# A fused attention and two-layer-block kernel: the second unit of w_out and the first block's y change places at the start of the third stage

## The chip, the cores and the metric

The kernel runs on one core of a Trainium2 chip. The metric is the device time in microseconds of one execution. A core has a matrix engine (TensorE, PE in the profile, with its weight loads as PEld), a vector engine (VectorE, DVE), a scalar engine (ScalarE, ACT), GpSimd (POOL) and a sync engine (SyncE, SP) that issues nearly all of this kernel's transfers.

## The reference

All inputs are float32, random. Attention is followed by two feed-forward blocks over 2304 tokens:

```python
scores = q @ k.T / 8                # 4 batches, 8 heads, 576 positions, 64 wide
scores = where(mask, scores, -1e9)  # heads 0-3: the last 32 positions; 4-7: every 32nd
x = softmax(scores) @ v             # reordered to (2304, 512)
h = ((x @ w1) * (x @ w2)) @ w3      # 512 -> 1024 -> 1024
y = h @ w_out                       # 1024 -> 512
h = y @ moe2_w_in                   # 512 -> 2048
g = h * sigmoid(1.702 * h)
out = g @ moe2_w_out                # 2048 -> 512
```

## The kernel before

**Numbers.** Every float32 operand is split into a high and a low part of type fp32r (`split_hi` on ScalarE, line 246; `split_lo` on VectorE, line 252), and a product is three matmuls (`ORDER`). Weights arrive as 64-bit words, which are turned into float32 by two ScalarE operations (a scaled copy of each half) and three VectorE operations.

**Stages.** The first two stages do attention, fold `w3` with the first `w_out`, and compute the first block for batches 0 to 2. The result y goes to DRAM (`ydram`). The third stage (`steps3`) does the first block for batch 3: for each half `hb` of its tokens eight passes `m`. A pass is two groups of twelve matmuls (`first`, line 716; places `at` and `at + 1`), a copy of the first group's sum (`copy`, `abf`, ScalarE, at + 0.99), a multiply (`mult`, VectorE, at + 1.99) and the split of the product into `ab` (at + 2.4, at + 2.75). Their PSUM tiles come from a pool of four (`mm`), so a group can start when the group four before it was copied or multiplied. Passes stand at 24 hb + 2 m; at 24 hb + 16 the product with the folded weight follows (`fourth`, line 1352). Places -8 to 0 hold the last such product of batch 2 (line 1173).

Beside these matmuls the third stage prepares the fourth: (a) the first block of y (768 tokens) in two halves `kk`: `y_load` fetches a half, and the nine steps of `y_steps` form sums and split them into `yq`; (b) the second `w_out` in eight units: `wo_load(u)` fetches 1 MB, and the fourteen steps of `wo_steps` convert it (two ScalarE, three VectorE operations), form sums and differences of its quarters, split them and store both parts in `tdram`. Unit 0 is done in the second stage, units 1 to 6 in the third, and unit 7 in the fourth. A unit's high parts are written over its raw tile, the low parts over the half of `sums` that holds the sums; so a raw tile is free when its store has ended. Raw tiles are lent by three rooms: `cv_a`'s `raw` and `x`, and `cv_b`'s `raw`. The second step of `y_steps` needs `x` too.

The fourth stage multiplies y with `w_in` units (`W[n]`, fetched from `widram`, split by ScalarE and VectorE) and the result, after the gelu, with the units in `tdram`, in three blocks of eight quads (`Quad`) and a sweep. A quad is 7 products (line 1496) and 2 pieces (line 1507). The `tdram` units come through a ring of eight tiles (`t_more` issues the next k loads). In a quad ScalarE copies partial sums out of PSUM (`keep`: s1, u1, z1; line 1559), and the next product into the same PSUM tile waits for that copy.

**Order.** Each stage is a list of (place, function). `written` sorts the list by place and emits the functions in that order; each engine then runs its own instructions strictly in that order, and SP its transfers. The places don't delay anything: an engine goes on as soon as its next instruction's inputs, and its output's room, are free. The third stage's places are groups of twelve matmuls; the fourth's are about a microsecond (a quad is 9.49).

At the end of the second stage `early_y` (line 1282) opens the pool `cv_a` and starts both loads of y: half 0 into `cv_a`'s raw tile, half 1 into one half of `sums`. `yq` is in a pool opened after the pools of the second stage (`cv`, `xbs`) were closed.

Of the kernel before, what the change touches and what calls it, by code (L numbers as in the profile page):

```python
# [16 lines left out]
I64 = mybir.dt.int64  # L17
# [4 lines left out]
P = 128  # L22
# [22 lines left out]
CW2 = 1024  # L45
# [4 lines left out]
NU = 8  # L50
# [162 lines left out]
def body(ctx: ExitStack, tc, qk, vv, mask, ql, vl, qs, vs, qmask, w1, w2, w3t, wo, win, wout, out):  # L213
    nc = tc.nc

    def pool(name, bufs=1, stack=ctx, **kw):
        return stack.enter_context(tc.tile_pool(name=name, bufs=bufs, reuse_waits="tile", **kw))
# [100 lines left out]
    def room(what, n, w, tag, bufs):  # L318
        if what + str(n) in lent:
            return lent[what + str(n)]  # L320
        return aq.tile([P, w], F32, tag=tag, name=tag, bufs=bufs)
# [186 lines left out]
    at = aps = None  # L508
# [760 lines left out]
    cv_a = None  # L1269
    early = {}  # L1270
    ys = {}

    def y_load(b, kk, room=None):
        t = room() if room else cv_a.tile([P, CW2], I64, tag="raw", name="raw")
        t = t.bitcast(F32)[:, :2 * BT]
        nc.sync.dma_start(
            t.rearrange("p (h n) -> p h n", h=2),
            ydram[kk::2, :, b * BT:(b + 1) * BT].rearrange("h p n -> p h n"),
        )
        return t  # L1280

    def early_y():
        nonlocal cv_a
        right0.close()
        cv_a = pool("cva", stack=right1, side="right")
        early["sums"] = cv_a.tile([P, 2, 7 * 256], F32, tag="hl", name="sums")
        ys[0] = y_load(0, 0)
        ys[1] = y_load(0, 1, lambda: early["sums"][:, 0])

    def early_load():  # L1290
# [3 lines left out]
    def early_room():  # L1294
        if 1 not in early:
            early[1] = cv[0].tile([P, 2 * CW2], F32, tag="x", name="x", bufs=2)
        return early[1]

    steps2 += [(27.0, early_load), (38.6, early_y)]
    steps2 += [(EARLY_AT + g, f) for g, f in wo_steps(0, lambda: early[0], early_room, None, 1.6)]  # L1300
    written(steps2)
# [8 lines left out]
    def y_steps(kk, ts):  # L1310

        q = {}

        def begin():
            q.update({n: ts[kk][:, n * HT:(n + 1) * HT] for n in range(4)})

        def first_two():
            begin()
            x = q["x"] = cv_a.tile([P, 2 * CW2], F32, tag="x", name="x")[:, :4 * HT]
            q.update({4 + n: x[:, n * HT:(n + 1) * HT] for n in range(4)})  # L1320
            t = ts[kk].rearrange("p (n t) -> p n t", t=HT)
            nc.vector.tensor_tensor(
                x.rearrange("p (m n t) -> p n m t", n=2, t=HT)[:, 0], t.rearrange("p (n m) t -> p m n t", m=2)[:, 1], t[:, :2], op=ALU.subtract,
            )

        def sum_(o, l, r, op):
            nc.vector.tensor_tensor(q[o], q[l], q[r], op=op)

        out = [first_two, lambda: sum_(5, 4, 3, ALU.subtract), lambda: sum_(7, 2, 5, ALU.add)]
        for lo, hi, src in ((0, 1, lambda: q[0]), (1, 3, lambda: ts[kk][:, 2 * HT:]), (3, 7, lambda: q["x"])):  # L1330
            view = lambda src=src: src().rearrange("p (n t) -> p n t", t=HT)
            out.append(lambda lo=lo, hi=hi, view=view: split_hi(yq[:, lo:hi, kk, 0], view()))
            out.append(lambda lo=lo, hi=hi, view=view: split_lo(yq[:, lo:hi, kk, 1], view(), yq[:, lo:hi, kk, 0]))
        return out
# [32 lines left out]
    steps3 = [(at - 48, f) for at, f in over]  # L1367
    for hb in range(2):
# [5 lines left out]
    rooms = (  # L1374
        lambda: cv_a.tile([P, CW2], I64, tag="raw", name="raw"),
        lambda: cv_b.tile([P, CW2], I64, tag="raw", name="raw"),
        lambda: cv_a.tile([P, CW2], I64, tag="x", name="x"),
    )
    sums = early["sums"]
    for kk, at in ((0, -4.6), (1, -1.6)):  # L1380
        gaps = (0.05, 1.0, 1.4, 0.1, 0.75, 0.8, 1.85, 2.0, 2.85)
        steps3 += [(at + g, f) for g, f in zip(gaps, y_steps(kk, ys))]

    todo3 = {}

    def wo_load(u):
        todo3[u] = rooms[(1, 0, 2)[(u - 1) % 3] if u < NU - 1 else 0]()
        nc.sync.dma_start(todo3[u], wout[u])

    UNIT = 7.2  # L1390
    for u in range(1, NU):
        at = 0.6 + UNIT * (u - 1)
        if u < NU - 1:
            steps3.append(((-7, -1.5, 1.4)[u - 1] if u < 4 else at - 2 * UNIT + 0.2, lambda u=u: wo_load(u)))
        if u < NU - 1:
            steps3 += [(at + g, f) for g, f in wo_steps(u, lambda u=u: todo3[u], lambda u=u: sums[:, u % 2])]
    for n, (lo, hi, a, b, c) in enumerate(((4, 6, 32.1, 40.2, 41.6), (5, 7, 40.05, 46.9, 47.7))):
# [47 lines left out]
    def do(at, f, *args, **kw):  # L1445
        steps4.append((at, lambda: f(*args, **kw)))
# [88 lines left out]
    QUAD = 7 * MM + 2 * PC  # L1535
# [144 lines left out]
    late = [f for _, f in wo_steps(NU - 1, lambda: todo3[NU - 1], todo3_lo, todo3_hi)]  # L1680
    at_late = (1.65, 2 + 1.65 / QUAD)
    for f, (i, t) in zip(late, (
        (1, 1.7), (2, 1.7), (2, 3.5), (2, 3.6), (3, 3.5), (3, 3.6), (4, 3.5), (4, 3.55),
        (4, 9.2), (5, 1.7), (5, 3.5), (5, 3.55), (5, 3.6), (5, 5.9),
    )):
        do(i * QUAD + t, f)
# [2 lines left out]

    do(-0.9, t_more, 2)  # L1690
    do(-0.8, W[2].fetch_in_place)
    do(-0.7, t_more, 2)
    do(-0.6, W[3].fetch_in_place)
    do(-0.55, wo_load, NU - 1)
    do(-0.5, t_more, 4)
    for b in range(NB):
        X, Y = [None] * 2, [None] * 2

# [6 lines left out]
        for i in range(NU):  # L1705
            q = Quad(b, i, X, Y, q)
            n = b * NU + i
            at = b * BLOCK + i * QUAD
# [46 lines left out]
```

## Time and profile before

| what | us |
|---|---|
| median of 3 runs | 808.64 (806.70 to 808.92) |
| the profiled execution | 806.77 |
| its span | 805.0 |
| TensorE busy in it | 774.4 |
| VectorE busy | 580.6 |
| ScalarE busy | 480.5 |

The mean granted TensorE clock is 0.992 of full speed. The profile gives the busy time of each engine, the chain of work that ended last, and for idle time of an engine what ended it. "L716" is line 716 of the kernel; `ps<-xal,w` is an instruction that writes `ps` and reads `xal` and `w`. SPq is SP's transfer queue; a transfer's row there is the time of its issue, not of its landing.

### The profile page before, as it was taken

How to read it: one execution, taken by the hardware profiler on the slowest of the kernel's cores; microseconds unless marked ns; L12 is line 12 of the kernel's file. 1: busy time of each engine (PE TensorE's matmuls, PEld its weight loads, DVE VectorE, ACT ScalarE, POOL GpSimd, SP SyncE). 2: the span in 40 equal slices, each digit the busy share in tenths (PEclk: the TensorE clock that was granted, in tenths of full speed). 3: DMA queues.
4: the chain of work that ended last, by engine and by line, in shares of the span. 5: the costliest groups of instructions: out<-in, count | busy, mean ns of one | idle time of the engine just before them, and what ended most of it. 6: DMA issues, size and time to landing. Idle time of an engine off the chain costs nothing.

```text
span 805.0 us, 16757 instructions
## 1 busy us (share of the span) xinstructions
PE 774.4 (96%) x6545; PEld 750.4 (93%) x6545; DVE 580.6 (72%) x1248; ACT 480.5 (60%) x1041; POOL 5.8 (1%) x14
## 2 busy tenths in 40 slices
PE   5899999999999999979999699999999999999997
PEld 4899999978999999879999699999999999999997
DVE  4999678788787787948785487796566795567743
ACT  5878565576665465444565467774566673666552
POOL 2000000000000000000000000000000000000000
PEclk9999999999999999999999899999999999999999
DMA  8976555541877463477999626789444489343382
GB/s 274 322 283 223 199 156 184 177 156 58 278 260 268 160 218 135 152 197 204 237 292 254 267 89 204 305 291 348 159 171 161 147 286 370 128 151 118 116 271 85
DMA packets 72062, 168.14 MB, mean 209 GB/s; under 512 B 6320, under 2 KB 45232, under 8 KB 69424
## 3 DMA queue, kind: packets, MB, share of 16 engines
q1 hardware_dynamic: 71840, 167.04, 62.4%
q8 instruction: 51, 0.84, 0.4%
q14 instruction: 27, 0.22, 0.1%
q10 hardware_dynamic: 144, 0.04, 0.0%
HBM read 130.88 MB, written 36.18 MB: 208 GB/s over the span
## 4 chain that ended last, share of the span: by engine, by line
PE 77%; DMA 8%; DVE 8%; ACT 4%; issue 2%; SPq 1%; ACTq 0%; DVEq 0%
PE acc L1507 22%; PE ps L1496 21%; PE ps L716 16%; PE ps L1173 8%; PE acc L1352 3%; PE acc L1019 3%; DMA raw<-in_w 2%; DMA w<-tdram 1%; DMA tdram<-x 1%; PE sc L533 1%; DVE w L252 1%; DVE xw L809 1%; PE pv L602 1%; DMA abdram<-abf 1%; ACT w L246 1%
## 5 line engine op out<-in xcount | busy, mean ns | idle before, releaser
L1507 PE MATMUL acc<-w,sp 128*128 128x256 f32 x1512 | 188.8, 283 | 0.0
L1507 PEld LDWEIGHTS acc<-w,sp 128*128 128x128 f32 x1512 | 186.7, 191 | 0.4 <-DVE sp L252 0.4
L1496 PE MATMUL ps<-yq,hl 128*128 128x384 f32 x924 | 167.9, 335 | 0.0
L1496 PEld LDWEIGHTS ps<-yq,hl 128*128 128x128 f32 x924 | 158.7, 188 | 0.6 <-DVE part L1452 0.6
L252 DVE TENSOR_TENSOR sp<-part,sp 128x384 fp32r<-128x384 f32 x144 | 75.5, 554 | 69.3 <-ACT sp L246 69.3
L716 PE MATMUL ps<-xah,w 128*128 128x288 f32 x512 | 103.2, 297 | 0.0
L716 PE MATMUL ps<-xbh,w 128*128 128x288 f32 x512 | 102.5, 295 | 0.3 <-DVE w L252 0.2
L716 PEld LDWEIGHTS ps<-xah,w 128*128 128x128 f32 x512 | 82.9, 190 | 0.0
L716 PE MATMUL ps<-xal,w 128*128 128x288 f32 x256 | 77.3, 302 | 5.8 <-ACT abf L1234 3.4
L1173 PE MATMUL ps<-ab,w 128*128 128x288 f32 x576 | 81.0, 300 | 1.8 <-DVE ab L252 1.8
L716 PEld LDWEIGHTS ps<-xbh,w 128*128 128x128 f32 x512 | 81.9, 188 | 0.8 <-DVE w L252 0.7
L1173 PEld LDWEIGHTS ps<-ab,w 128*128 128x128 f32 x576 | 78.3, 192 | 3.2 <-DVE ab L252 2.3
L246 ACT ACTIVATE sp<-part 128x384 fp32r<-128x384 f32 x144 | 68.3, 518 | 16.4 <-PE acc L1507 15.7
L716 PE MATMUL ps<-xbl,w 128*128 128x288 f32 x256 | 77.0, 301 | 0.0
L1449 ACT ACTIVATE part<-part 128x384 f32<-128x384 f32 x72 | 37.8, 526 | 60.5 <-DVE part L1452 60.5
L716 PEld LDWEIGHTS ps<-xal,w 128*128 128x128 f32 x256 | 48.5, 190 | 7.4 <-ACT abf L1234 3.7
L246 ACT ACTIVATE ab<-abf 128x288 fp32r<-128x288 f32 x64 | 27.3, 439 | 42.4 <-DVE abf L1237 40.0
L716 PEld LDWEIGHTS ps<-xbl,w 128*128 128x128 f32 x256 | 48.1, 188 | 0.9
L1019 PE MATMUL acc<-w,w 128*128 128x512 f32 x192 | 45.5, 396 | 0.2
L1019 PEld LDWEIGHTS acc<-w,w 128*128 128x128 f32 x192 | 35.9, 189 | 9.1 <-ACT raw L1025 1.0
L252 DVE TENSOR_TENSOR hl<-fetched,hl 128x1024 fp32r<-128x1024 f32 (+1 forms) x40 | 43.3, 1083 | 0.0
L246 ACT ACTIVATE w<-xw 128x512 fp32r<-128x512 f32 (+1 forms) x30 | 23.2, 774 | 29.6 <-DVE xw L809 28.8
(189 smaller groups left out, 1095.6 us busy)
## 6 DMA issues: line engine op xcount, KB each, us to landing
w<-tdram SPq DMA_DIRECT2D x84, 512.0 KB, 4.2
fetched<-widram SPq DMA_DIRECT2D x20, 896.0 KB, 7.7
raw<-in_win SPq DMA_DIRECT2D x8, 1024.0 KB, 5.5
widram<-x SPq DMA_DIRECT2D x8, 896.0 KB, 5.5
raw<-in_wout SPq DMA_DIRECT2D x6, 1024.0 KB, 6.3
tdram<-sums SPq DMA_DIRECT2D x6, 896.0 KB
raw<-in_w3t SPq DMA_DIRECT2D x10, 512.0 KB, 4.8
abf<-abdram SPq DMA_DIRECT2D x32, 144.0 KB, 4.2
```

The source lines that it names most:

```text
L246: nc.scalar.activation(hi, src, AF.Copy)
L252: e.tensor_tensor(lo, src, r(hi), op=ALU.subtract)
L533: nc.tensor.matmul(sc[:nq, g, i * P:i * P + nk], qs[rows, i], ks[rows, i], start=True, stop=True,)
L602: nc.tensor.matmul(pv[rows, h // 2, :nq], L["v"][:nk, h * D:(h + 1) * D], ps[:nk, h * nq:(h + 1) * nq], start=True, stop=True,)
L716: nc.tensor.matmul(ps, ws[a][m // 2][:, at:at + P], xh[c][:, k, cols], start=(k == 0 and (a, c) == ORDER[0]), stop=(k == KC - 1 and (a, c) ...
L809: "e": lambda xf, rf, ri, ru, x, hi, lo: nc.vector.tensor_tensor(x, x, ri[:, :, 0], op=ALU.add),
L1019: nc.tensor.matmul(acc[f], hl[:, a, f * P:(f + 1) * P], wor[c][g], start=(g == 0 and (a, c) == ORDER[0]), stop=(g == MC - 1 and (a, c) == ...
L1173: nc.tensor.matmul(yacc[n], wfs[a][k][:, n * P:(n + 1) * P], hold[s % 2, k][:, c], start=(k == 0 and (a, c) == ORDER[0]), stop=(k == MC - ...
L1352: nc.tensor.matmul(st[0], wfs[a][k][:, n * P:(n + 1) * P], hold[hb, k][:, c], start=(k == 0 and (a, c) == ORDER[0]), stop=(k == MC - 1 and ...
L1449: nc.scalar.activation(out(), src(), func)
L1496: nc.tensor.matmul(ps, w[a][:, f * 256 + kk * P:f * 256 + (kk + 1) * P], yq[:, b, kk, c], start=(first and kk == 0 and (a, c) == ORDER[0]) ...
L1507: nc.tensor.matmul(to, g.t[:, a, t * P:(t + 1) * P], t3[:, i % 2, c], start=(opens and i == 0 and n == 0 and t % 2 == 0), stop=(i == NU - ...
```

## The change

The load of unit 1 takes the place, in `early_y`, that the load of y's half 0 had, and the tile. Y's half 0 is loaded at place -6.9 of the third stage into `cv_b`'s raw tile, where unit 1's load had been at -7. Unit 1's steps move from 0.6 to -5.8. Y's half 1 is worked first, from -0.9 (it was the second, from -1.6), and half 0 from 2.2 (it was the first, from -4.6). Units 2 to 6 stand at 6 + 7.2 (u - 2), that is 1.8 places earlier, and their loads have new places and rooms.

At the start of the fourth stage the load of unit 7 stands before that of `W[3]`, and the third to sixth ring loads stand behind both. Unit 7's first conversion goes from place 1.7 to 9.2 of quad 1.

```diff
--- before.py
+++ after.py
@@ -1269,6 +1269,7 @@
     cv_a = None
     early = {}
     ys = {}
+    todo3 = {}
 
     def y_load(b, kk, room=None):
         t = room() if room else cv_a.tile([P, CW2], I64, tag="raw", name="raw")
@@ -1284,7 +1285,8 @@
         right0.close()
         cv_a = pool("cva", stack=right1, side="right")
         early["sums"] = cv_a.tile([P, 2, 7 * 256], F32, tag="hl", name="sums")
-        ys[0] = y_load(0, 0)
+        todo3[1] = cv_a.tile([P, CW2], I64, tag="raw", name="raw")
+        nc.sync.dma_start(todo3[1], wout[1])
         ys[1] = y_load(0, 1, lambda: early["sums"][:, 0])
 
     def early_load():
@@ -1377,21 +1379,20 @@
         lambda: cv_a.tile([P, CW2], I64, tag="x", name="x"),
     )
     sums = early["sums"]
-    for kk, at in ((0, -4.6), (1, -1.6)):
+    steps3.append((-6.9, lambda: ys.update({0: y_load(0, 0, rooms[1])})))
+    for kk, at in ((1, -0.9), (0, 2.2)):
         gaps = (0.05, 1.0, 1.4, 0.1, 0.75, 0.8, 1.85, 2.0, 2.85)
         steps3 += [(at + g, f) for g, f in zip(gaps, y_steps(kk, ys))]
 
-    todo3 = {}
-
     def wo_load(u):
-        todo3[u] = rooms[(1, 0, 2)[(u - 1) % 3] if u < NU - 1 else 0]()
+        todo3[u] = rooms[(0, 1, 2, 0, 1, 0)[u - 2]]()
         nc.sync.dma_start(todo3[u], wout[u])
 
     UNIT = 7.2
     for u in range(1, NU):
-        at = 0.6 + UNIT * (u - 1)
-        if u < NU - 1:
-            steps3.append(((-7, -1.5, 1.4)[u - 1] if u < 4 else at - 2 * UNIT + 0.2, lambda u=u: wo_load(u)))
+        at = -5.8 if u == 1 else 6 + UNIT * (u - 2)
+        if 1 < u < NU - 1:
+            steps3.append((((2.6, 5.5, 5.7)[u - 2] if u < 5 else at - 10), lambda u=u: wo_load(u)))
         if u < NU - 1:
             steps3 += [(at + g, f) for g, f in wo_steps(u, lambda u=u: todo3[u], lambda u=u: sums[:, u % 2])]
     for n, (lo, hi, a, b, c) in enumerate(((4, 6, 32.1, 40.2, 41.6), (5, 7, 40.05, 46.9, 47.7))):
@@ -1680,7 +1681,7 @@
     late = [f for _, f in wo_steps(NU - 1, lambda: todo3[NU - 1], todo3_lo, todo3_hi)]
     at_late = (1.65, 2 + 1.65 / QUAD)
     for f, (i, t) in zip(late, (
-        (1, 1.7), (2, 1.7), (2, 3.5), (2, 3.6), (3, 3.5), (3, 3.6), (4, 3.5), (4, 3.55),
+        (1, 9.2), (2, 1.7), (2, 3.5), (2, 3.6), (3, 3.5), (3, 3.6), (4, 3.5), (4, 3.55),
         (4, 9.2), (5, 1.7), (5, 3.5), (5, 3.55), (5, 3.6), (5, 5.9),
     )):
         do(i * QUAD + t, f)
@@ -1689,10 +1690,10 @@
 
     do(-0.9, t_more, 2)
     do(-0.8, W[2].fetch_in_place)
-    do(-0.7, t_more, 2)
+    do(-0.7, wo_load, NU - 1)
     do(-0.6, W[3].fetch_in_place)
-    do(-0.55, wo_load, NU - 1)
-    do(-0.5, t_more, 4)
+    do(6.0, t_more, 2)
+    do(QUAD + 6, t_more, 4)
     for b in range(NB):
         X, Y = [None] * 2, [None] * 2
```

## Rows read from the trace of the kernel before

**Rows 1.** The page, part 1: busy us (share of the span), instructions.

```profile
PE 774.4 (96%) x6545; PEld 750.4 (93%) x6545; DVE 580.6 (72%) x1248; ACT 480.5 (60%) x1041; POOL 5.8 (1%) x14
```

**Rows 2.** TensorE's waits, 333 to 480: line, releaser: us total, times, longest.

```profile
PE ps L1496 <- ACT u L1559: 6.8, 1, 6.8
PE ps L716 <- ACT abf L1234: 3.4, 1, 3.4
...
PE ps L716 <- DVE abf L1237: 1.3, 2, 0.9
PE ps L716 <- ACT ysb L1181: 1.1, 1, 1.1
```

**Rows 3.** Busy time by stretch; after POOL: granted clock, DMA share, GB/s.

```profile
362.00:366.00 4.00, 3.57 (x17) 3.22 (x17) 3.93 (x7) 0.74 (x2) 0.00 (x0) 0.57 0.73 266
```

**Rows 4.** The chain that ended last, 318 to 462: start us, us, what.

```profile
340.66 9.39 DMA tdram<-x
...
396.23 25.60 PE ps L716 x192
...
434.52 5.24 PE ps L1496 x30
...
454.66 3.82 PE ps L1496 x12
```

**Rows 5.** ScalarE in order of time: start us, us, operation [idle before].

```profile
339.25 0.39 ACT L1181 ACTIVATE ysb<-ps 128x288 f32<-128x288 f32 x1
350.15 0.52 ACT L246 ACTIVATE yq<-raw 128x384 fp32r<-128x384 f32 x1 [10.52 <-DMA tdram<-x]
...
360.63 0.39 ACT L1234 ACTIVATE abf<-ps 128x288 f32<-128x288 f32 x1
...
452.72 1.10 ACT L1144 ACTIVATE raw<-raw 128x1024 int32<-128x1024 uint32 x1 [8.51 <-DMA w<-tdram]
...
473.45 0.47 ACT L1559 ACTIVATE u<-ps 128x384 f32<-128x384 f32 x1
```

**Rows 6.** VectorE in order of time, 330 to 462.

```profile
340.55 0.95 DVE L1322 TENSOR_TENSOR x<-raw 128x768 f32<-128x768 f32 x1
...
355.68 0.96 DVE L1322 TENSOR_TENSOR x<-sums 128x768 f32<-128x768 f32 x1
...
359.72 1.76 DVE L252 TENSOR_TENSOR yq<-x,yq 128x1536 fp32r<-128x1536 f32 x1 [0.68 <-ACT yq L246]
361.40 0.69 DVE L1146 TENSOR_SCALAR sums<-sums 128x1024 int32<-128x1024 int32 x1
...
367.81 1.09 DVE L252 TENSOR_TENSOR sums<-sums,raw 128x896 fp32r<-128x896 f32 x1 [0.71 <-ACT raw L246]
```

**Rows 7.** SP's queue in order of time: start us, us to issue, transfer.

```profile
330.81 0.38 SPq L1276 DMA_DIRECT2D raw<-ydram  x1
...
341.11 1.35 SPq L1388 DMA_DIRECT2D raw<-in_wout  x1
...
368.98 0.37 SPq L1128 DMA_DIRECT2D tdram<-raw  x1
...
374.39 0.34 SPq L1388 DMA_DIRECT2D raw<-in_wout  x1
...
440.88 1.02 SPq L1388 DMA_DIRECT2D raw<-in_wout  x1
...
443.01 0.52 SPq L1340 DMA_DIRECT2D fetched<-widram  x1
```

**Rows 8.** TensorE in order of time, 349 to 354 and 460 to 476.

```profile
349.78 0.29 PE L716 MATMUL ps<-xal,w 128*128 128x288 f32 x1
...
475.09 1.21 PE L1496 MATMUL ps<-yq,hl 128*128 128x384 f32 x6
```

**Rows 9.** DMA issues at 374 and at 443: KB each, us to landing.

```profile
raw<-in_wout SPq DMA_DIRECT2D x1, 1024.0 KB, 7.4
...
fetched<-widram SPq DMA_DIRECT2D x1, 896.0 KB, 14.4
```

## The prediction

> **What bounds the kernel now.** The page comes first: TensorE is busy for 774.4 of 805.0 us [rows 1], so a change pays only where TensorE waits or runs at its lower clock. Second come TensorE's waits from 333 us, where the third stage begins, to 480 us, inside the fourth [rows 2]: 3.4, 1.3 and 1.1 us in the third stage, 6.8 us at the start of the fourth. (A wait of 1.8 us behind `ab`, left out of the rows, ends before the first moved step and stays.) Third is the granted clock: 0.57 from 362 to 366 us [rows 3], that is 2.4 GHz fallen to 1.2 for most of these 4 us, just after the 3.4 us wait. After the 6.8 us wait the chain shows twelve matmuls in 3.82 us, where thirty of them had taken 5.24, so twelve 2.10 [rows 4]. Last, ScalarE's order of work [rows 5] says why TensorE waits:
>
> 1. ScalarE is free at 339.6 and stands 10.5 us before the first split into `yq`, until the store `tdram<-x` has ended: 340.66 + 9.39 [rows 4]. What it waits for is the room of `yq`, where the closed pool's `x` was, and not the y data: VectorE reads the first y tile at 340.55 already [rows 6]. All of the y work is then squeezed in behind 350, ScalarE copies pass 0 only at 360.63, and TensorE has no free PSUM tile until then.
> 2. ScalarE stands 8.5 us before unit 7's first conversion, to 452.72 [rows 5]. That load was issued at 440.88 [rows 7], seventh in a burst of ten. The quad's copy `u`, which TensorE needs, is queued behind the conversion.
>
> **The third stage.** What can go is 3.4 + 1.3 + 1.1 = 5.8 us of waits, and of the 4 us at 0.57 the part 4 x 0.43 = 1.7 us: 7.5 us.
>
> Unit 1's load takes the SP slot of 330.81 [rows 7] and carries 1024 KB where y had 768. Y had landed by 340.55; a third more of these 9.7 us is 343.8 at the latest, and I take 340, since y had been there for a while. So unit 1's two conversions run from 340, ahead of y, and VectorE's part follows: in the trace it is 6.4 us from 361.40 to the low half at 367.81 [rows 6], with a multiply inside, and 2.2 us of low halves after it. From 341.7 that ends at about 350, just as the store releases `yq`. Unit 1 costs nothing: the hole of 10.5 us hides it. With the load at 343.8 it would end 4 us later, and y with it.
>
> The new order then has y's second half. Its first subtraction runs while `yq` is still held; the rest is what one half takes in the trace, 355.68 to 361.48 [rows 6], less that subtraction, 4.9 us, and half a microsecond for the first split: done at 355.6. Pass 0's copy now stands ahead of the big split and comes at 351.7. TensorE starts pass 0 at 349.78 [rows 8] and takes 25.60 / 16 = 1.60 us for a group of twelve matmuls [rows 4]; a pass is two groups, and with four PSUM tiles each group needs the tile of the fourth group before it. Pass 0's multiply, at 355.6 to 356.0, is in time for the group due at 357.8. Y's first half was loaded in the slot of 341.11 [rows 7], which had unit 1's larger transfer, and is read at 356. Multiply 1 is done at 359.1 (due 361.0), the half at 362.8, multiply 2 at 363.2 (due 364.1). So far no wait, by a margin that shrinks from 1.8 to 0.9 us.
>
> Unit 2's load carries the wait that I trust least. Its room is unit 1's tile, whose high half must have been stored. The store is issued at 348.8, behind what is left of unit 0's stores and y's load; a store like it let its tile go 374.39 - 368.98 = 5.4 us after issue [rows 7]. Counted from 350.05, where unit 0's store ends, that is 355.4. A load of this size lands in 7.4 us [rows 9]: 362.8. ScalarE comes to unit 2's conversion at 361.0 and waits 1.8 us. Behind it are pass 2's split and pass 3's copy, done at 365.3, due at 365.6. VectorE's multiply 3 follows at 367.6, 0.4 us late for TensorE; multiply 4 is 0.35 late and copy 5 0.65. That is 1.4 us. The bounds are none lost (the load lands by 361) and all 7.5. I take 1.4, because the store and the load are priced from rows of the same transfers: gain 6.1 us. Loads 3 and 4 wait on SP for VectorE's last reads of y, and nothing stands behind them there until unit 2's store, 4.6 places (7 us) on.
>
> After this, units 2 to 6 stand 1.8 places (2.9 us) earlier than before, and each load 7.1 places (11 us) or more ahead of its conversion. TensorE waited nowhere from 383 to 434 with the same work [rows 2], so this is put at nothing; were that cover gone, a late load would cost what unit 2's does.
>
> **The fourth stage.** SP runs down its list without pacing, so its order is what counts. Before: two ring tiles, W[2], two, W[3], unit 7, two, W[4]. After: two, W[2], unit 7, W[3], four ring tiles, W[4]. The bytes are the same, but unit 7 has 2 x 512 + 896 KB ahead of it and not 4 x 512 + 2 x 896. The burst's 6784 KB took from about 434.5 to 457.4, where W[4], its last, landed: issued at 443.01 [rows 7], 14.4 us to landing [rows 9]. At that pace unit 7 with what is ahead of it, 2944 KB, is in 9.9 us later, at 444.4. The first conversion moves to place 9.2 of quad 1; a quad is 9.5 places of a microsecond, so it comes at 434.5 [rows 4] + 9.5 + 9.2 = 453.2, 8.8 us after the load. The copy `u` now stands before it: the 6.8 us go, and 3.82 - 2.10 = 1.7 us of lower clock. The conversion, 1.1 us, pushes ScalarE's next items by at most its length; the next quad's `u` ends at 473.92 [rows 5] for a matmul at 475.09 [rows 8], 1.2 us in hand, so no cost. The ring tiles put back are read from place 32 of the stage on, and W[3], now one transfer later, is split at place 24: nothing. Gain 8.5 us; bounds 2.7 (rival B) and 8.5.
>
> Here a row and a rule bear on the same doubt. By order and bytes, 4864 KB of the burst, unit 7's load should have been in at about 451, and its reader started at 452.72 with a later issued ring load named as what ended last [rows 5]. The Trainium skill (DMA: Bandwidth & Descriptors, Queues, rings and completion order) says that the 16 engines each consume descriptors in ring order, but that completion is not first-in first-out per issuing engine. The trace agrees as far as it goes. By issue order the sum is the forecast's, by the rule at its worst B's.
>
> **The sum.** 6.1 + 8.5 = 14.6 us. The profiled execution took 806.77 us (span 805.0): 792.2. It is at the low end of the runs shown, 806.7 to 808.92; their median of 808.64 less 14.6 is 794.0. I say 793.0, between the two.
>
> **Rivals.**
> A. Unit 2's load comes 3 us after 362.8. For it: it shares the queue with unit 1's second store. Against: 1.8 us of waiting are counted already. TensorE would wait 3 us more, about as long as the wait that brought the clock down, and pay those 1.7 us too: gain 14.6 - 4.7, 797.
> B. Unit 7's load lands last of the burst, at 457.4. ScalarE would wait 4.2 us at 453.2, `u` of the next quad would be 4.2 + 1.1 - 1.2 = 4.1 us late for its matmul, with the clock 5.8: 792.2 + 5.8 = 798. For it: completion out of order is what the row above leaves open. Against: three transfers are ahead of it and not nine.
> C. The third stage's waits move and don't go. VectorE has the same instructions and is busy for 3.93 of 4 us at 362 to 366 [rows 3]; y's first half is merely the later one. TensorE would lose the 7.5 us in small pieces behind multiplies: 806.77 - 8.5 = 798.3. Against: unit 1's 8 us of VectorE do move into an empty hole.
> D. Slower. Unit 2's load stands at the head of SP's queue for unit 1's store, and ScalarE behind the load. If the two took not 12.8 but 26 us, pass 3's copy would come at 378.5, TensorE would stand 13 us with four PSUM tiles full, and with the clock's 1.7 us the whole gain would be gone; beyond 26 us it is slower, 814 at 33 us. Against: 5.4 and 7.4 us in the rows, and no pair near twice that.
>
> **How the numbers follow.** The forecast gets 0.60, A 0.16, B 0.08, C 0.12, D 0.04. The range: with no new wait the profile gives 806.77 - 16.0 = 790.8, and a microsecond below for the runs' scatter is 789.5, rounded. Upwards it takes in A, B and C and the 1.9 us between profiled execution and median: 800.5. A measurement tells about 0.3% from no change, 2.4 us. A, B and C are all faster by more. D gives slower 0.04, and 0.03 of C's share is for a loss in the fourth stage beside it: same 0.03, faster 0.93.
>
> **What would show it.** Third stage: unit 1's conversion on ScalarE at about 340; ScalarE's idle time before `yq` near 1 us; no 3.4 us wait, the clock at 1.00 from 345 to 430, small waits behind `abf` only; the third stage's last-but-one product (L1352) begins near 377. The lower clock at 338 to 341 stays. Fourth stage: no wait behind `u`, unit 7's conversion without a DMA wait. I am wrong if `yq` is held past 350 by another transfer, if unit 2's conversion waits over 3 us, or if TensorE's wait comes back in quad 2.

## The result and the profile after

The changed kernel takes 799.09 us (median of 6 runs, 797.49 to 799.96), the kernel before 808.79 (6 runs, 806.70 to 811.0). The ratio is 0.9879, 95% interval 0.9860 to 0.9897: 9.7 us, where the forecast was 14.6 to 15.8. The time lies in the stated range (789.5 to 800.5), near its upper end, and beside rival C's 798.3. The profiled execution took 799.78 us, its span is 798.0.

TensorE's waits in the changed stages, first: line and releaser, us in total, times, longest.

```profile
PE ps L716 <- DVE abf L1237: 4.4, 5, 2.3
PE ps L1173 <- DVE ab L252: 1.8, 2, 1.1
PE ps L716 <- ACT abf L1234: 1.7, 3, 1.0
```

Against [rows 2] the 6.8 us behind `u` are gone, and so is the lower clock after it. The third stage still waits: 4.4 + 1.7 = 6.1 us where it had 5.8. Its clock no longer falls at 362 [rows 3], but its waits have spread to eight places.

Stage lengths say this best, because profiled executions differ by up to 4 us in reaching the third stage (its first mark is at 336.87 us before and at 338.64 after, with the same matmuls ahead of it). Four marks are read from TensorE's rows in order of time (start us, us, instruction, idle before it): the first wait behind `ab`, the start of the stage's two products with the folded weight, and the fourth stage's first product. After:

```profile
338.64 0.66 PE L1173 MATMUL ps<-ab,w 128*128 128x288 f32 x3 [1.10 <-DVE ab L252]
...
383.37 12.85 PE L1354 MATMUL acc<-ab,w 128*128 128x288 f32 x96
...
424.00 12.75 PE L1354 MATMUL acc<-ab,w 128*128 128x288 f32 x96
...
436.58 1.58 PE L1497 MATMUL ps<-yq,w 128*128 128x384 f32 x8
```

The same marks for every kernel of this study (differences of such rows; the fourth stage runs from its first product to the end of the span):

| kernel | mark to first product | first to second | third stage in all | fourth stage |
|---|---|---|---|---|
| before | 46.49 | 38.31 | 97.49 | 370.64 |
| after | 44.73 | 40.63 | 97.94 | 361.42 |
| s4_alone | 46.38 | 38.31 | 97.38 | 361.22 |
| s3_alone | 44.22 | 40.09 | 97.01 | 369.13 |
| ysb4 | 39.53 | 41.17 | 93.39 | 361.22 |
| load5 | 45.05 | 38.45 | 96.19 | 361.20 |
| both | 39.95 | 38.44 | 91.09 | 361.26 |
| ysb_before | 46.64 | 38.19 | 97.41 | 370.36 |
| s4_place | 46.14 | 38.30 | 97.14 | 362.06 |
| s4_order | 46.36 | 38.20 | 97.25 | 363.03 |
| yload | 43.13 | 40.39 | 96.22 | 361.72 |

Kernels with the same third stage agree within 0.4 us in its columns where it is the old one (`before`, `s4_alone`, `s4_place`, `s4_order`) and within 1 us where it is the new one (`after`, `s3_alone`); these are single executions, and differences of that size say nothing.

The fourth stage is 9.2 us shorter. The third gains 1.8 us up to its first product, and loses 2.3 between the two products.

ScalarE in order of time shows where the first part went:

```profile
341.02 1.17 ACT L1144 ACTIVATE raw<-raw 128x1024 int32<-128x1024 uint32 x1
342.08 0.39 ACT L1181 ACTIVATE ysb<-ps 128x288 f32<-128x288 f32 x1
342.37 1.12 ACT L1145 ACTIVATE sums<-raw 128x1024 f32<-128x1024 f32 x1
345.39 0.41 ACT L1181 ACTIVATE ysb<-ps 128x288 f32<-128x288 f32 x1 [1.90 <-PE ps L1173]
348.47 0.95 ACT L246 ACTIVATE raw<-sums 128x896 fp32r<-128x896 f32 x1 [2.68 <-DVE sums L1133]
353.65 0.41 ACT L1181 ACTIVATE ysb<-ps 128x288 f32<-128x288 f32 x1 [4.22 <-DMA ydram<-ysb]
353.96 0.95 ACT L246 ACTIVATE raw<-sums 128x896 fp32r<-128x896 f32 x1
354.80 1.25 ACT L246 ACTIVATE yq<-sums 128x384 fp32r<-128x384 f32 x2
...
369.30 1.14 ACT L1144 ACTIVATE raw<-raw 128x1024 int32<-128x1024 uint32 x1 [2.28 <-DMA raw<-in_wout]
...
406.22 1.13 ACT L1145 ACTIVATE sums<-raw 128x1024 f32<-128x1024 f32 x1 [2.07 <-DMA tdram<-sums]
```

Unit 1 is converted at 341 and moves into the old 10.5 us hole [rows 5], as said. But between its two high halves stands the third copy of batch 2's last y (`y_out`, line 1181). There are two `ysb` tiles; the third copy needs the first one back, whose store was queued behind unit 0's two stores and y's load. The chain of waits has it, with y's load as SP issues it (line 1277) and the transfers that follow (start us, us):

```profile
342.88 1.37 SPq L1277
...
344.31 9.26 DMA ydram<-ysb
...
354.93 5.48 DMA tdram<-raw
...
360.43 8.77 DMA raw<-in_wout
...
393.01 13.19 DMA tdram<-sums
```

The forecast's times stand on the trace before, whose first mark is 1.8 us earlier, so they are compared from each trace's own mark: y's split starts 16.2 us after it and not 13.2 (350.1), unit 1's store 16.3 and not 11.9 (348.8), and unit 2's load lands at 30.6 and not 25.9 (362.8).

In the fourth stage unit 7's conversion waits for nothing:

```profile
453.28 1.16 ACT L1144 ACTIVATE raw<-raw 128x1024 int32<-128x1024 uint32 x1
```

### The profile page after: what moved, and what is told of

Its sections match the earlier page's. It is cut to its first block, busy times and chain, and to the rows that moved or that the text cites. A ratio compares the mean times of both kernels' runs of the same rounds, so it can differ in the third digit from the quotient of the medians.

```text
span 798.0 us, 16759 instructions
## 1 busy us (share of the span) xinstructions
PE 771.7 (97%) x6545; PEld 746.6 (94%) x6545; DVE 580.8 (73%) x1248; ACT 480.2 (60%) x1041; POOL 5.8 (1%) x14
## 4 chain that ended last, share of the span: by engine, by line
PE 75%; DMA 12%; DVE 6%; ACT 4%; issue 2%; SPq 0%; ACTq 0%; DVEq 0%
PE acc L1508 23%; PE ps L1497 22%; PE ps L716 12%; PE ps L1173 8%; PE acc L1019 5%; DMA raw<-in_w 3%; DMA raw<-in_wout 2%; DMA tdram<-sums 2%; PE acc L1354 2%; DMA ydram<-ysb 1%; DMA vl<-in_vl 1%; PE sc L533 1%; PE pv L602 1%; ACT sm L556 1%; DMA tdram<-raw 1%
## 5 line engine op out<-in xcount | busy, mean ns | idle before, releaser
L246 ACT ACTIVATE sp<-part 128x384 fp32r<-128x384 f32 x144 | 68.2, 518 | 16.4 <-PE acc L1508 15.7
```

The lines of the kernel that those rows point to most:

```text
L246: nc.scalar.activation(hi, src, AF.Copy)
```

## The experiments

In theory 1, the forecast, both parts of the change gain. In theory 2, formed from the trace after, the fourth stage gives all of it, the third being held by two waits: for the y copy's tile at 350, and for the room of unit 5's sums at 406. The rival to theory 2 says that VectorE's lag or the busy queue holds the stage, whatever waits. The ratios are to the kernel before, run on the same chip.

**The parts alone.** `s4_alone` is the kernel before with the last two hunks of the change, `s3_alone` with all but these.

> The kernel before with the fourth stage's part of the change alone (unit 7's load ahead of W[3]'s, two groups of ring loads behind it, unit 7's first conversion at place 9.2). Both theories: TensorE's wait of 6.8 us behind u and the 1.7 us at the lower clock go. Theory 1 (the forecast, each part gives its own gain): 8.5 us under the kernel before. Theory 2 (the trace after shows all of the gain here): 9 to 10 us under it, as the whole change.

> The kernel before with the third stage's part alone. Theory 1 (the forecast): about 6 us under the kernel before. Theory 2: the stage keeps its length, because ScalarE, in the middle of unit 1, waits for the tile of y's copy and starts y's split at about 354 instead of 350, and units 2 and 5 wait for transfers: within 1 us of the kernel before.

Measured: `s4_alone` 799.15 us, ratio 0.9888 (0.9859 to 0.9916); `s3_alone` 809.12 us, ratio 1.0005 (0.9984 to 1.0025). The fourth stage's part is the whole gain. The third's, alone, has its wait too, in ScalarE's list:

```profile
ACT ysb L1181 <- DMA ydram<-ysb: 4.7, 1, 4.7
```

**The tile.** `ysb4` is the changed kernel with

```diff
-        ysb = where[n % len(where)].tile([P, HB], F32, tag="ysb", name="ysb", bufs=2)
+        tag, bufs = ("abf", 3) if s == 5 and n > 1 else ("ysb", 2)
+        ysb = where[n % len(where)].tile([P, HB], F32, tag=tag, name="ysb", bufs=bufs)
```

> The changed kernel, with the third and fourth copy of the last y of batch 2 written to a tile of the pool's other kind (abf), so that they wait for no store. Theory 2: ScalarE's 4.2 us wait goes, y's split starts when yq is released by the store of unit 0, at 351 to 352 of the span and not 354.8, and TensorE's 2.3 us wait behind the multiply shrinks to under 1: 2 to 3 us under the changed kernel. Rival (the DMA queue itself holds the stage until it drains near 353.5, whatever tile is waited for): y's split starts at 353.5 or later and the gain is under 1 us.

Measured: 794.64 us, ratio 0.9831 (0.9804 to 0.9857). ScalarE in it:

```profile
349.09 0.39 ACT L1182 ACTIVATE ysb<-ps 128x288 f32<-128x288 f32 x1
...
351.77 1.26 ACT L246 ACTIVATE yq<-sums 128x384 fp32r<-128x384 f32 x2 [1.45 <-DMA tdram<-x]
...
363.83 1.15 ACT L1144 ACTIVATE raw<-raw 128x1024 int32<-128x1024 uint32 x1 [1.29 <-DMA raw<-in_wout]
```

The copy waits for nothing, y's split starts 13.4 us after the mark, 2.8 earlier than in the changed kernel, and now waits for the store that holds `yq`, as before the change. The first product comes 5.2 us sooner in the stage than after (39.53 against 44.73), more than the 2 to 3 us expected: the whole 2.3 us wait of TensorE goes, and unit 2's chain of store and load is earlier as well. The rival falls: with the queue as busy, the tile alone made the difference. Nor was it the clock, which is the same in both profiles: 0.83 from 336 to 346 us and 1.00 from there to 362.

The same edit in the kernel before, `ysb_before`:

> The kernel before with the two y copies in tiles of the other kind, and nothing else. Theory 2 (before the change ScalarE's hole of 10.5 us hides the wait for the tile, which became the bound only with the change): within 1 us of the kernel before. Rival (the tile costs 4 us whatever the order): 4 us under it.

Measured: 807.63 us, ratio 0.9994 (0.9980 to 1.0007). The tile cost nothing there; ScalarE stands for `yq` in any case:

```profile
352.98 0.52 ACT L246 ACTIVATE yq<-raw 128x384 fp32r<-128x384 f32 x1 [10.67 <-DMA tdram<-x]
```

In the kernel before, the first copy's store and the third copy were these (SP's queue, the issue's KB and us to landing, ScalarE):

```profile
342.51 11.98 SPq L1182 DMA_DIRECT2D ydram<-ysb  x3
...
ydram<-ysb SPq DMA_DIRECT2D x1, 144.0 KB, 10.2
...
353.76 0.39 ACT L1181 ACTIVATE ysb<-ps 128x288 f32<-128x288 f32 x1
```

The store let the tile go at 352.7, a microsecond before ScalarE came to the copy.

**What is queued ahead of the tile's store.** `yload` puts y's half 0 behind the first two y copies:

```diff
-    steps3.append((-6.9, lambda: ys.update({0: y_load(0, 0, rooms[1])})))
+    steps3.append((-3.9, lambda: ys.update({0: y_load(0, 0, rooms[1])})))
```

> The changed kernel with the load of y's half 0 at place -3.9, behind the first two copies of y in SP's order, not ahead of them. Theory 2 with the queue as its cause: the store of the first copy has 768 KB less ahead of it, some 3 us, so ScalarE's 4.2 us wait for its tile shrinks to about 1 and y's split starts at 352 of a span like that of the changed kernel: the third stage 2 to 3 us shorter. Rival (the store's time has nothing to do with what is queued ahead, or y's half 0 is now late itself): the third stage keeps its 97.9 us.

Measured: 798.97 us, ratio 0.9891 (0.9865 to 0.9917), so not to be told from the changed kernel by its time. The third stage is 96.22 us, 1.7 shorter than after and 0.8 shorter than in `s3_alone`, and ScalarE's wait 2.6 us (4.2 after, 4.7 in `s3_alone`). ScalarE's row, and the chain's for the store:

```profile
351.93 0.41 ACT L1181 ACTIVATE ysb<-ps 128x288 f32<-128x288 f32 x1 [2.58 <-DMA ydram<-ysb]
...
343.03 8.82 DMA ydram<-ysb
```

This is half of what was expected, and most of it is not the 768 KB. The store was issued at 343.03 and not 344.31, because SP no longer spent 1.4 us on issuing y's load ahead of it; it then took 8.8 us instead of 9.3. So taking the bytes of y's load from ahead of it gave about 0.4 us. That unit 0's two stores, still ahead of it, make the rest is likely, but was not tried.

**The room of unit 5's sums.** In SP's order after, unit 5's load (place 17.6) stands between the two stores of unit 3 (17.55 and 18.6):

```profile
391.73 0.36 SPq L1128 DMA_DIRECT2D tdram<-raw  x1
392.18 0.51 SPq L1389 DMA_DIRECT2D raw<-in_wout  x1
393.01 0.85 SPq L1128 DMA_DIRECT2D tdram<-sums  x1
```

The second store ends 13.19 us after its issue, and unit 5 needs its half of `sums`. `load5`, which moves unit 6's load as well, is the changed kernel with

```diff
-            steps3.append((((2.6, 5.5, 5.7)[u - 2] if u < 5 else at - 10), lambda u=u: wo_load(u)))
+            steps3.append((((2.6, 5.5, 5.7)[u - 2] if u < 5 else at - 2 * UNIT + 0.2), lambda u=u: wo_load(u)))
```

> The changed kernel with the loads of units 5 and 6 put 14.2 places ahead of their unit, as before the change, not 10. Theory 2: the second store of unit 3, which takes 13.2 us behind unit 5's load, lands sooner, ScalarE's 2.1 us wait before unit 5's second conversion goes, and TensorE's three waits at 411 to 416 (1.55 us in all) with it: 1.5 us under the changed kernel. Rival (VectorE's lag, not the transfer, makes these waits): unchanged within 0.5 us.

Measured: 796.74 us, ratio 0.9859 (0.9833 to 0.9886). By its time alone it can't be told from the changed kernel, whose interval overlaps with this one; the rows tell it. First product to second takes 38.45 us, as before the change, against 40.63: 2.2 us. Unit 5's second conversion follows its first without a wait:

```profile
404.02 1.13 ACT L1144 ACTIVATE raw<-raw 128x1024 int32<-128x1024 uint32 x1
405.05 1.12 ACT L1145 ACTIVATE sums<-raw 128x1024 f32<-128x1024 f32 x1
```

**Both edits.**

> The changed kernel with both edits that paid by themselves: the two y copies in tiles of the other kind, and the loads of units 5 and 6 at 14.2 places ahead. Theory 2 (two separate waits, one at 350, one at 406): the gains add, 4.4 + 2.4 us under the changed kernel, near 792.5, which is the forecast of the third stage made good. Rival (both only shorten one lag of VectorE): 794.6, as with the tiles alone.

Measured: 794.14 us, ratio 0.9816 (0.9796 to 0.9836); it is the fastest here, but its time is nearer to the rival's 794.6 than to the 792.5 expected and can't be told from that of `ysb4`. The stage lengths can: each edit acts in its own column of the table, 44.73 to 39.95 and 40.63 to 38.44, and the third stage takes 91.09 us, 6.4 under before. (Its profiled execution reached the first mark at 340.65, 2.3 us later than that of `ysb4`, which is why the spans are equal at 793.0; whether that is chance, the runs don't show.) What TensorE still waits for:

```profile
PE ps L1173 <- DVE ab L252: 1.8, 2, 1.1
PE ps L716 <- DVE abf L1238: 1.0, 2, 0.6
PE ps L716 <- ACT abf L1235: 0.8, 2, 0.6
```

**The fourth stage's two edits, one at a time.**

> The kernel before with unit 7's first conversion at place 9.2 of quad 1 and the old order of loads. In the trace before, the load let the conversion go 18.4 us after the fourth stage's start, and in the new place ScalarE comes to it 16.7 us after that start. Theory 1: it waits some 1.7 us, of which 1.2 are in hand: 8 to 9 us under the kernel before, the place alone is enough. Rival (the load needs its new position too): 3 us or more of the wait stay, 4 to 6 us under it.

> The kernel before with the new order of loads and the first conversion where it was, at place 1.7 of quad 1, which ScalarE reaches 9.8 us after the stage's start. Theory 1 (loads land by issue order and bytes, unit 7 at 9.9 us): no wait, 8 us under the kernel before. Rival B (unit 7's load lands near the burst's end, 16 us or later): ScalarE waits 6 us, TensorE 4 and the clock falls: 1 to 3 us under it.

Measured: `s4_place` 799.55 us, ratio 0.9892 (0.9875 to 0.9909); `s4_order` 801.05 us, ratio 0.9919 (0.9896 to 0.9943). The first conversion in each, ScalarE's row:

```profile
453.11 1.17 ACT L1144 ACTIVATE raw<-raw 128x1024 int32<-128x1024 uint32 x1 [0.66 <-DMA raw<-in_wout]
```

```profile
447.68 1.10 ACT L1144 ACTIVATE raw<-raw 128x1024 int32<-128x1024 uint32 x1 [3.46 <-DMA raw<-in_wout]
```

Each does most of it. With the place alone, and so with the old order, the load lands 17.5 us after the stage's start and ScalarE waits 0.7 us. The wait is put down to unit 7's own load here, not to a ring load as in [rows 5]; the forecast's pace has the 4864 KB up to it in at 16.4 us. With the order alone it lands at 12.8 us (447.68 less the stage's start at 434.87), between theory 1's 9.9 and rival B's 16, and TensorE waits 1.8 us behind `u`. About 1 of the 3 us beyond theory 1 is a late start: SP issued the burst's first transfer 1.05 us after the stage's start.

```profile
435.92 1.95 SPq L1435 DMA_DIRECT2D w<-tdram  x2
```

Fourth stage: 8.6 us shorter, 7.6, and with both 9.2 to 9.4.

## Why the prediction was right, and where it was wrong

**The fourth stage was right.** Forecast 8.5 us; 9.2 in the profile, and `s4_alone` timed at 0.9888 is 9.1 us. `u` no longer waits, and unit 7's conversion follows without a DMA wait. Rival B did not come about, but in `s4_order` the load was 3 us later than bytes and order gave; the place of the conversion, which `s4_place` shows to be nearly enough by itself (it leaves TensorE a wait of 0.7 us), covered that. About half a microsecond that I had not counted lies in the stage's first quad, where ScalarE's copy `z` waited 1.1 us for a store of y before the change. It is gone in `s4_place`, `s4_order` and in `s3_alone` too, so neither edit of the fourth stage was needed for it; its cause stays open.

**The third stage was wrong in two steps of its working.** It was to gain 6.1 us; `s3_alone` shows no gain by its time (1.0005). That the total still lies in the range is partly luck: the range reached up to 800.5 for rivals whose mechanisms are not what happened.

1. "Unit 1 costs nothing: the hole of 10.5 us hides it." The hole hid one thing more. Before the change, too, the third y copy needed the tile of the first, and the store that held it took 10.2 us, to 352.7; but ScalarE, held to 350.15 by the wait for `yq`, came to that copy only at 353.76, so it never showed as a wait. When unit 1 went into the hole, the y copy that stands in the middle of unit 1 waited 4.2 us, and y, unit 1's store and unit 2's load moved with it. The prices were near: the store took 5.5 us where 5.4 were said, unit 2's load 8.8 where 7.4 were; their start was wrong. `ysb4` shows it: with that wait gone the stage up to its first product is 6.96 us shorter than before (46.49 to 39.53), where I had forecast 6.1.
2. "After this, units 2 to 6 ... so this is put at nothing". I had checked that each load comes early enough for its own reader. I had not checked what each load is put ahead of: unit 5's load stood before unit 3's second store, which held the sums' room. It cost 2.3 us. `load5` takes it away.

The two losses, 4.8 and 2.2 us by the columns of `both`, make up, to about 0.1 us, what separates 97.94 from its 91.09 us. 97.49 - 6.1 = 91.4 had been the forecast.

**The rivals.** A put the risk at the right transfer: unit 2's load landed 4.6 us later than said, counted from the mark. But its cause lay ahead of it, in the tile. C's number was right and its reason wrong: VectorE's lag was not the cause, since one tile and one order of loads gave the stage back. D was far off.

**Its own marks.** From the mark, unit 1's conversion was to come at about 3.1 us and came at 2.4; the last-but-one product was to begin at 40.1 and began at 44.7, wrong by 4.6. The clock is 1.00 from 346 on, as said. "I am wrong if `yq` is held past 350 by another transfer" came true in effect: y's split was held by another transfer, though through ScalarE's y copy and not through the room of `yq`. Unit 2's conversion waited 2.3 us, under the 3 of its sign.

## What to carry to other kernels

A hole in an engine's time can hide several waits; before work is moved into it, list what each instruction that then runs early needs, output tiles and their pending stores too, not only the wait that the profile names. When a load is moved in a transfer queue, look also at what now stands behind it and who needs that back.

## What the runs showed of the hardware

On SP's queue transfers issued behind large ones were late. 144 KB of y took 9.3 us from issue to landing behind unit 0's two stores and y's load, 8.8 with that load behind it (`yload`), and 10.2 in the kernel before, where the same bytes issued at 351.0, after unit 0's stores had ended, took 2.1. 896 KB took 13.2 us behind a store and a load, where a store of the same size, with no other large transfer just ahead of it, let its tile go in 5.4 [rows 7].

The clock's fall is not fixed by the instructions. Near the first mark, with the same matmuls and the same 1.8 us of waits, the mean granted clock from 336 to 346 us was 0.83 in four profiles (before, after, `ysb4`, `s4_order`) and 1.00 in the other seven. It did not set the stage's length: `ysb4` with the fall took 39.53 us to its first product, `both` without it 39.95. Behind the same 2.3 us wait at 362, the clock fell to 0.53 and 0.61 from 364 to 368 in `load5`, and stayed at 1.00 in after and `s3_alone`. So the forecast's 1.7 us of clock in the third stage can come and go.
